# SSD, GLU and a top-1 mixture of experts on one core: the order of TensorE written out from GLU block 7 to the second expert's early rows

## Chip, cores and metric

The kernel runs on one core of a Trainium2 chip. The metric is the device time of one execution in microseconds; lower is better. Times come from the runs, durations and waits from one profiled execution.

## Reference

Three stages follow each other. A state-space layer (x, a, B, C in float32; 4 batches, 8 heads, 768 positions, head size 32, state size 16) gives 3072 tokens of 256 numbers. A gated layer follows, and then a mixture of eight experts in which each token goes to one expert:

```python
gate = 1.0 / (1.0 + np.exp(-(x @ w_gate)))
val = x @ w_val
x = (gate * val @ w_out).astype(np.float32)
...
expert_idx = np.argmax(logits, axis=1)
...
for e in range(E):
    mask = expert_idx == e
    h = np.maximum(x[mask] @ w1[e], 0.0)
    out[mask] = gate_w[mask, None] * (h @ w2[e])
```

w_gate and w_val are 256 x 1536, w_out is 1536 x 256, w1 is 256 x 1024 and w2 1024 x 256 for each expert. logits are cosine similarities of token and expert embedding over tau, gate_w is the softmax weight of the chosen expert.

## The kernel before

**Products.** Each float32 operand is split into a high and a low part (fp32r), and each product is three matmuls (high by high, high by low, low by high), so a contraction over 256 takes six.

**GLU steps.** The 3072 tokens are eight blocks (0 to 7) of 384. A block has twelve steps, one for each 128 columns of the hidden layer: step s is block s // 12, column tile s % 12. A step has a gate group (gate_step, six matmuls of 384 columns into bank 0, L583; ScalarE's tanh gives th, L587), a val group (val_step, six into bank 1, L597; VectorE gives pf, L601, ScalarE the high part of p, L604, VectorE its low part, L609) and an out group (out_step, nine of 264 columns into banks 2 to 4, L619), which uses the p of two steps earlier. In blocks 0 to 6 the state-space work of the next block stands among the steps.

**Routing.** After a block, route_a and route_b (VectorE, small instructions) find the expert of each token. route_rank counts with six tiny matmuls (L694, L695) how many earlier tokens go to the same expert, and needs ohb and car (L666, L671) from VectorE. route_c makes slot numbers from it (sli, L729), and GpSimd writes the block's rows, with the gate weight (row, L677), in three indirect DMAs into a table xs in DRAM (L735). For block 6 the rank is called in step 92 and the matmul of make_bump (L758) in step 94; for block 7 the rank is called in expert work, after up step 3 of the first segment.

**Expert work.** It has ten segments: segs[0] and segs[1] are the first 256 rows of experts 0 and 1 (the early rows, filled by blocks 0 to 6), segs[2] and segs[3] their next 192 rows, segs[4] to segs[9] the 448 rows of experts 2 to 7. seg_load brings the rows from xs on chip (xr, L832; it waits for the scatters) and copies gate weight and token number out of them on VectorE (gt, L839). seg_transpose turns them for one half k of the 256 columns (L855, bank 6 or 7), ScalarE and VectorE split the result (xt, L858 and L859). Eight up steps follow (L870: six matmuls into bank 0 or 1 in turn; ScalarE and VectorE give h, L874 and L875), and eight down steps (L884: six matmuls for segs[0] to segs[3], into banks 2 and 3 or 4 and 5). The results leave as yo (L919) with an indirect DMA. Weights of the experts come in 64 loads into three buffers stg (L798, SyncE's queue) and are split into we by ScalarE and VectorE (L806, L807); that runs from block 7 on.

**What sets the order.** Engines run their instructions in the order in which they stand. A list scheduler, with a timeline of its own, sets this order from the program, but within tc.manual_schedule the engines named keep the order of the code. Before, steps 28 to 83 (blocks 2, from its step 4, to 6) are such a region for TensorE (`"man": [[28, 84, ["PE"]]]` in the table of numbers); from step 84, block 7's first, the scheduler chooses. pend holds the up steps whose down step is still to come:

```python
for j, sg in enumerate(segs):
    ...
    for f in range(NFE):
        ...
        up_step(sg, f, hall[f] if last and f < NQ else None)
        ...
        pend.append((sg, f))
        while len(pend) > (kn("dlag", 2) if sg["ws"] != WS_A + WS_B else kn("dlag2", 1)):
            down_next()
        tf = kn("tfs", [2, 5, 5, 5, 5])[min(j, 4)]
        if f in (tf, tf + 1) and not last:
            seg_transpose(segs[j + 1], f - tf)
```

The table has "dlag": 1 and no "tfs", "dlag2", "m2" or "m2a", so the defaults in the code hold for these.

Of the kernel before, what the change touches and what calls it, by code (L numbers as in the profile page):

```python
# [3 lines left out]
def kn(n, d):  # L4
    return KN.get(n, d)
# [24 lines left out]
KD = DM // P  # L30
# [10 lines left out]
def kernel(  # L41
# [1102 lines left out]
    for s in range(S0, nstep + LAG2):  # L1144
        t, f = divmod(s, NF)
        if s == kn("trunc", 999):
            att_cm.__exit__(None, None, None)
            return
        if s == S0 + HOLD:
            hold.close()  # L1150
        for m in kn("man", []):
            if s == m[0]:
                region = tc.manual_schedule(engines={getattr(ET, e) for e in m[2]})
                region.__enter__()
            if s == m[1]:
                region.__exit__(None, None, None)
        if s == nstep - NF:
            close_att()
        if s > nstep - NF:
            with ExitStack() as es:  # L1160
                if kn("wl", 1) < 99:
                    for m in marks[min(s - kn("wl", 1), nstep - 1)]:
                        es.enter_context(tc.issue_after(m))
                weight_step()
        if s == nstep - 1:
            seg_load(segs[0])
            seg_load(segs[1])
        run(s, 0)
        drip()
        if s < nstep:  # L1170
            go(gate_step(t, f))
        run(s, 1)
        drip(2)
        gov = kn("gov", 999) <= s
        if s < nstep and not gov:
            go(val_step(t, f))
        run(s, 2)
        drip()
        while len(outs_done) <= s - (LAG if s < 26 else LAG2):
            out_step(*divmod(len(outs_done), NF))  # L1180
            outs_done.append(s)
        if s < nstep and gov:
            go(val_step(t, f))
        run(s, 3)
        drip(2)
# [21 lines left out]
                    seg_out(sg, i)  # L1207

    for j, sg in enumerate(segs):
        if j == kn("m2a", 0) and kn("m2", 0):  # L1210
            region = tc.manual_schedule(engines={ET.PE})
            region.__enter__()
        if j == kn("m2", 0) and j:
            region.__exit__(None, None, None)
        if j == 0:
            for k in range(KD):
                seg_transpose(sg, k)
            load_expert(2, main, slots[2])
        last = j == len(segs) - 1
        if last:  # L1220
# [1 line left out]
        for f in range(NFE):  # L1222
            if f == 0 and 2 <= j + 1 < len(segs):
                seg_load(segs[j + 1])
            up_step(sg, f, hall[f] if last and f < NQ else None)
            if j == 0:
                drip(10)
                if f == 3:
                    route_rank(NBLK - 1)
                if f == 4:  # L1230
                    route_c(NBLK - 1)
            pend.append((sg, f))
            while len(pend) > (kn("dlag", 2) if sg["ws"] != WS_A + WS_B else kn("dlag2", 1)):
                down_next()
            tf = kn("tfs", [2, 5, 5, 5, 5])[min(j, 4)]
            if f in (tf, tf + 1) and not last:
                seg_transpose(segs[j + 1], f - tf)
            weight_step()
        if last:
            while pend:  # L1240
                down_next()
            with tc.manual_schedule(engines={mybir.EngineType.PE}):
                for i in range(1, len(sg["ws"])):
                    for f in range(NFE):
                        down_tile(sg, f, i)
                    seg_out(sg, i)
# [52 lines left out]
```

## Time and profile before

| | |
|---|---|
| runs | 574.83, 579.59, 579.90 us (median 579.59) |
| profiled execution, its own time | 576.94 us |
| its span, first to last instruction | 575.2 us (1.7 us lie around it) |
| mean granted TensorE clock | 0.99 of 2.4 GHz |
| TensorE busy | 553.6 us |
| VectorE, ScalarE, GpSimd busy | 345.3, 282.4, 153.4 us |
| HBM traffic, mean | 130 GB/s |

All times in rows are microseconds from the first instruction. A matmul's duration is its passage through the array, in which several overlap: six gate matmuls of 0.34 us start within 1.05 us. So the time that a group takes is read from start to start. Busy counts these overlapping passages once.

### The profile page before, as it was taken

Reading aid. Unit: us, or ns where it says so; the run is one execution under the profiler, and the core shown is the slowest. Engines: PE = TensorE matmul, PEld = TensorE weight load, DVE = VectorE, ACT = ScalarE, POOL = GpSimd, SP = SyncE. Lnnn points to the kernel's source line nnn. Section 1 sums busy time; section 2 is a strip of 40 time slices with the busy share of each in tenths; the row PEclk is TensorE's granted clock in tenths of the full one; section 3 lists DMA queues with packets and bytes.
Section 4 is the critical chain, followed back from the end, with each engine's and each line's share of the span. In section 5 each row is a group of like instructions: output and inputs, shape, how many; then the busy total and the mean of one; then the engine's idle time right before and its main releaser. Section 6 shows DMA issues by size and latency. Waiting matters only on the chain. (4 is left out here: it accounts for less than half of the span.)

```text
span 575.2 us, 11363 instructions
## 1 busy us (share of the span) xinstructions
PE 553.6 (96%) x4160; PEld 521.1 (91%) x4160; DVE 345.3 (60%) x984; ACT 282.4 (49%) x712; POOL 153.4 (27%) x176
## 2 busy tenths in 40 slices
PE   9799999999999999999999999999999999999993
PEld 6689889999899999999999999999899889999993
DVE  4799966546747447547446447787376556543241
ACT  7566656355446446446445335673365444523220
POOL 3587843122432032231231020202221021121122
PEclk9799999999999999999999999999999999999998
DMA  8689799481561481471360131671365254200000
GB/s 282 172 291 268 213 238 288 144 186 52 175 175 37 120 199 41 135 175 38 92 147 3 33 106 37 204 225 59 120 189 179 74 172 149 87 29 10 18 26 30
DMA packets 74947, 75.02 MB, mean 130 GB/s; under 512 B 4971, under 2 KB 68659, under 8 KB 74888
## 3 DMA queue, kind: packets, MB, share of 16 engines
q1 hardware_dynamic: 72120, 67.91, 41.7%
q0 software_dynamic: 2688, 6.32, 3.3%
q8 instruction: 33, 0.54, 0.4%
q14 instruction: 26, 0.21, 0.1%
q10 hardware_dynamic: 80, 0.03, 0.0%
HBM read 58.53 MB, written 16.24 MB: 130 GB/s over the span
## 5 line engine op out<-in xcount | busy, mean ns | idle before, releaser
L619 PE MATMUL bk<-w,p 128*128 128x264 f32 x864 | 121.4, 285 | 0.0
L597 PE MATMUL bk<-xt,w 128*128 128x384 f32 x576 | 119.6, 343 | 1.0 <-DVE pf L601 1.0
L583 PE MATMUL bk<-xt,w 128*128 128x384 f32 x576 | 119.9, 343 | 0.0
L619 PEld LDWEIGHTS bk<-w,p 128*128 128x128 f32 x864 | 116.0, 188 | 0.4 <-issue 0.2
L597 PEld LDWEIGHTS bk<-xt,w 128*128 128x128 f32 x576 | 99.1, 189 | 3.1 <-DVE pf L601 1.2
L583 PEld LDWEIGHTS bk<-xt,w 128*128 128x128 f32 x576 | 98.6, 190 | 0.4
L604 ACT ACTIVATE p<-pf 128x384 fp32r<-128x384 f32 x96 | 50.0, 521 | 88.8 <-DVE pf L601 88.8
L870 PE MATMUL bk<-xt,we 128*128 128x448 f32 (+2 forms) x480 | 92.3, 330 | 0.0
L601 DVE SCALAR_TENSOR_TENSOR pf<-th,bk 128x384 f32<-128x384 f32 x96 | 53.0, 552 | 51.0 <-PE bk L597 44.9
L870 PEld LDWEIGHTS bk<-xt,we 128*128 128x128 f32 x480 | 78.0, 188 | 4.3
L587 ACT ACTIVATE th<-bk 128x384 f32<-128x384 f32 x96 | 46.7, 487 | 51.3 <-PE bk L583 51.2
L609 DVE TENSOR_TENSOR p<-pf,p 128x384 fp32r<-128x384 f32 x87 | 51.4, 590 | 32.6 <-ACT p L604 32.0
L874 ACT ACTIVATE h<-bk 128x448 fp32r<-128x448 f32 (+2 forms) x74 | 34.4, 464 | 71.9 <-PE bk L870 69.1
L920 POOL DMA_INDIRECT out_dram<-yo,gt x32 | 32.1, 1003 | 133.6 <-DVE yo L919 127.2
L875 DVE SCALAR_TENSOR_TENSOR h<-bk,h 128x448 fp32r<-128x448 f32 (+2 forms) x74 | 38.5, 521 | 38.3 <-ACT h L874 36.7
L312 POOL TENSOR_SCALAR_AFFINE_SELECT l<-l 128x512 f32<-128x512 f32 x42 | 27.4, 655 | 126.0 <-ACT l L308 108.2
L896 PE MATMUL bk<-h,we 128*128 128x448 f32 x240 | 58.0, 372 | 0.9 <-DVE h L875 0.9
L308 ACT ACTIVATE l<-cb,ncol 128x128 f32<-128x128 f32 x168 | 53.4, 390 | 9.6 <-DVE m L327 9.5
L735 POOL DMA_INDIRECT xs<-row,sli x24 | 25.4, 1057 | 89.5 <-DVE sli L729 29.5
L807 DVE TENSOR_TENSOR we<-stg,we 128x512 fp32r<-128x512 f32 x64 | 43.0, 685 | 9.2 <-ACT we L806 9.2
L896 PEld LDWEIGHTS bk<-h,we 128*128 128x128 f32 x240 | 43.6, 188 | 4.8 <-DVE h L875 1.6
L806 ACT ACTIVATE we<-stg 128x512 fp32r<-128x512 f32 x64 | 39.3, 627 | 16.8 <-PE bk L896 12.0
(171 smaller groups left out, 598.3 us busy)
## 6 DMA issues: line engine op xcount, KB each, us to landing
stg<-in_w_dram SPq DMA_DIRECT2D x64, 256.0 KB, 3.2
cb<-cum_d SPq DMA_DIRECT2D x21, 512.0 KB, 5.7
hl_d<-hl SPq DMA_DIRECT2D x7, 768.0 KB, 4.2
bts<-hl_d SPq DMA_DIRECT2D x21, 192.0 KB, 5.4
cts<-hl_d SPq DMA_DIRECT2D x42, 96.0 KB, 6.5
xs<-z SPq DMA_DIRECT2D x4, 903.0 KB, 8.7
raw<-in_w_val_dram SPq DMA_DIRECT2D x6, 512.0 KB, 5.6
xn<-in_x_dram SPq DMA_DIRECT2D x8, 384.0 KB, 5.3
```

Source lines behind the costliest of these rows:

```text
L308: A.activation(out=l[:, k, :], in_=cb[h], func=AF.Exp, bias=ncol[:, b, h, c:c + 1], scale=1.0)
L583: gi = T.matmul(gp, lhsT=wt["g", f // 2][:, wq, k, (f % 2) * P:(f % 2 + 1) * P], rhs=xts[t][:, xq, k, 0:TB], start=(i == 0), stop=(i == 3 ...
L587: A.activation(out=th, in_=gp, func=AF.Tanh, scale=0.5)
L597: T.matmul(vp, lhsT=wt["v", f // 2][:, wq, k, (f % 2) * P:(f % 2 + 1) * P], rhs=xts[t][:, xq, k, 0:TB], start=(i == 0), stop=(i == 3 * KD ...
L601: vi = V.scalar_tensor_tensor(out=pf, in0=ths.pop((t, f)), scalar=1.0, in1=vp, op0=ALU.add, op1=ALU.mult)
L604: ai = A.activation(out=p[:, 0, 0:TB], in_=pf, func=AF.Copy)
L609: pi = V.tensor_tensor(out=p[:, 1, 0:TB], in0=pf, in1=p[:, 0, 0:TB].bitcast(F32), op=ALU.subtract)
L619: T.matmul(oacc[t, i], lhsT=p[:, pq, i * P:(i + 1) * P], rhs=wt["o", f // 2][:, wq, f % 2, :], start=(f == 0 and j == 0), stop=(f == NF - ...
L806: A.activation(out=w[:, 0], in_=st[j][:, i], func=AF.Copy)
L807: V.tensor_tensor(out=w[:, 1], in0=st[j][:, i], in1=w[:, 0].bitcast(F32), op=ALU.subtract)
L870: T.matmul(hp[:, 0:W], lhsT=we[sg["e"], 0, f // 2][:, wq, k, (f % 2) * P:(f % 2 + 1) * P], rhs=sg["xt"][:, xq, k, 0:W], start=(i == 0), st ...
L896: T.matmul(sg["o", k][:, 0:W], lhsT=we[sg["e"], 1, f // 2][:, wq, f % 2, k * P:(k + 1) * P], rhs=sg["h", f][:, pq, 0:W], start=(f == 0 and ...
```

## The change

The region in which TensorE keeps the order of the code no longer ends at step 84; it begins at step 28 (S0) as before and ends ahead of segs[2], so it takes in block 7 and segs[0] and segs[1]. In that stretch code order now counts, and some of it is written in another way: the transposes of segs[0] stand in the loop of steps, behind the val group of the last step and ahead of the last two out groups; those of the next segment stand ahead of the down step in place of behind it; segs[2] is transposed at up steps 6 and 7 of segs[1] in place of 5 and 6; in segs[1] the down steps are two up steps behind in place of one, and one is caught up at its end. The other numbers were the defaults or the table's, and stay.


```diff
--- before.py
+++ after.py
@@ -1148,12 +1148,9 @@
             return
         if s == S0 + HOLD:
             hold.close()
-        for m in kn("man", []):
-            if s == m[0]:
-                region = tc.manual_schedule(engines={getattr(ET, e) for e in m[2]})
-                region.__enter__()
-            if s == m[1]:
-                region.__exit__(None, None, None)
+        if s == S0:
+            region = tc.manual_schedule(engines={ET.PE})
+            region.__enter__()
         if s == nstep - NF:
             close_att()
         if s > nstep - NF:
@@ -1176,6 +1173,9 @@
             go(val_step(t, f))
         run(s, 2)
         drip()
+        if s == nstep:
+            for k in range(KD):
+                seg_transpose(segs[0], k)
         while len(outs_done) <= s - (LAG if s < 26 else LAG2):
             out_step(*divmod(len(outs_done), NF))
             outs_done.append(s)
@@ -1207,14 +1207,9 @@
                     seg_out(sg, i)
 
     for j, sg in enumerate(segs):
-        if j == kn("m2a", 0) and kn("m2", 0):
-            region = tc.manual_schedule(engines={ET.PE})
-            region.__enter__()
-        if j == kn("m2", 0) and j:
+        if j == 2:
             region.__exit__(None, None, None)
         if j == 0:
-            for k in range(KD):
-                seg_transpose(sg, k)
             load_expert(2, main, slots[2])
         last = j == len(segs) - 1
         if last:
@@ -1230,12 +1225,14 @@
                 if f == 4:
                     route_c(NBLK - 1)
             pend.append((sg, f))
-            while len(pend) > (kn("dlag", 2) if sg["ws"] != WS_A + WS_B else kn("dlag2", 1)):
-                down_next()
-            tf = kn("tfs", [2, 5, 5, 5, 5])[min(j, 4)]
+            tf = (2, 6, 5, 5, 5)[min(j, 4)]
             if f in (tf, tf + 1) and not last:
                 seg_transpose(segs[j + 1], f - tf)
+            while len(pend) > (2 if j == 1 else 1):
+                down_next()
             weight_step()
+        if j == 1:
+            down_next()
         if last:
             while pend:
                 down_next()
```

TensorE at block 6's rank (L694, L695; six matmuls into bank 7). Rows begin with the val group of a step: bk1_5030 is step 86's before, bk1_5240 step 91's now. Before:

```order
L597 MATMUL bk1_5030<-xt_4441,w_479 128x384 x6
L619 MATMUL bk2_5043<-w_457,p_4977 128x264 x2
L619 MATMUL bk3_5047<-w_457,p_4977 128x264 x2
L619 MATMUL bk4_5051<-w_457,p_4977 128x264 x2
L619 MATMUL bk2_5043<-w_457,p_4977 128x264
L619 MATMUL bk3_5047<-w_457,p_4977 128x264
L619 MATMUL bk4_5051<-w_457,p_4977 128x264
L694 LDWEIGHTS tri_115
L694 MATMUL bk7_5269<-ohb_5009,tri_115 128x8
L695 LDWEIGHTS oneb_82
L695 MATMUL bk7_5269<-car_5010,oneb_82 128x8
L694 LDWEIGHTS tri_115
```

Now:

```order
L597 MATMUL bk1_5240<-xt_4441,w_711 128x384 x6
L619 MATMUL bk2_5042<-w_599,p_5170 128x264 x3
L619 MATMUL bk3_5046<-w_599,p_5170 128x264 x3
L619 MATMUL bk4_5050<-w_599,p_5170 128x264 x3
L694 LDWEIGHTS tri_115
L694 MATMUL bk7_5268<-ohb_5008,tri_115 128x8
L695 LDWEIGHTS oneb_82
L695 MATMUL bk7_5268<-car_5009,oneb_82 128x8
L694 LDWEIGHTS tri_115
L694 MATMUL bk7_5268<-ohb_5008,tri_115 128x8
L695 LDWEIGHTS oneb_82
L695 MATMUL bk7_5268<-car_5009,oneb_82 128x8
```

The rank matmuls stand five steps later, and all six together: before, gate group 87 (bk0_5065) stood behind the first three of the six.

TensorE at the transposes of segs[0] (bk6_5490 before, bk6_5445 now). bk0_5276 and bk1_5285 are gate and val group of step 92, bk0_5323 and bk1_5334 of step 93, bk1_5423 is val group 95, the last. Before:

```order
L583 MATMUL bk0_5276<-xt_4441,w_771 128x384 x6
L855 MATMUL bk6_5490<-ident_84,xr_5407 128x128 x2
L597 MATMUL bk1_5285<-xt_4441,w_825 128x384 x6
L619 MATMUL bk2_5043<-w_748,p_5250 128x264 x2
L619 MATMUL bk3_5047<-w_748,p_5250 128x264 x2
L619 MATMUL bk4_5051<-w_748,p_5250 128x264 x2
L619 MATMUL bk2_5043<-w_748,p_5250 128x264
L619 MATMUL bk3_5047<-w_748,p_5250 128x264
L619 MATMUL bk4_5051<-w_748,p_5250 128x264
L583 MATMUL bk0_5323<-xt_4441,w_771 128x384 x6
L597 MATMUL bk1_5334<-xt_4441,w_825 128x384 x6
L855 MATMUL bk6_5490<-ident_84,xr_5407 128x128 x2
```

Now:

```order
L583 MATMUL bk0_5414<-xt_4441,w_972 128x384 x6
L597 MATMUL bk1_5423<-xt_4441,w_916 128x384 x6
L619 MATMUL bk2_5042<-w_890,p_5342 128x264 x3
L619 MATMUL bk3_5046<-w_890,p_5342 128x264 x3
L619 MATMUL bk4_5050<-w_890,p_5342 128x264 x3
L855 MATMUL bk6_5445<-ident_84,xr_5406 128x128 x4
L619 MATMUL bk2_5042<-w_1117,p_5394 128x264 x3
L619 MATMUL bk3_5046<-w_1117,p_5394 128x264 x3
L619 MATMUL bk4_5050<-w_1117,p_5394 128x264 x3
L619 MATMUL bk2_5042<-w_1117,p_5432 128x264 x3
L619 MATMUL bk3_5046<-w_1117,p_5432 128x264 x3
L619 MATMUL bk4_5050<-w_1117,p_5432 128x264 x3
```

The two halves stood behind gate group 92 and val group 93; they now stand together behind out group 93, which follows val group 95.

TensorE in segs[1]: bk0 and bk1 with 128x256 (L870) are its up steps, bk4 and bk5 its down steps. bk6_5843 and bk6_5846 are the transposes of segs[2], bk7_6212 and bk7_6206 those of one half of segs[4]. Before, from up step 4 on:

```order
L870 MATMUL bk0_5810<-xt_5583,we1_4920 128x256 x6
L855 MATMUL bk6_5843<-ident_84,xr_5730 128x96 x2
L884 MATMUL bk4_5770<-we2_4923,h_5801 128x256 x2
L884 MATMUL bk5_5774<-we2_4923,h_5801 128x256 x2
L884 MATMUL bk4_5770<-we2_4923,h_5801 128x256
L884 MATMUL bk5_5774<-we2_4923,h_5801 128x256
L870 MATMUL bk1_5826<-xt_5583,we1_4920 128x256 x6
L855 MATMUL bk7_6212<-ident_84,xr_6046 128x128 x2
L884 MATMUL bk4_5770<-we2_4924,h_5817 128x256 x2
```

Now, from down step 1 on (bk0_5803 is up step 4):

```order
L884 MATMUL bk4_5779<-we2_4921,h_5750 128x256 x3
L884 MATMUL bk5_5783<-we2_4921,h_5750 128x256 x3
L870 MATMUL bk0_5803<-xt_5576,we1_4919 128x256 x6
L884 MATMUL bk4_5779<-we2_4922,h_5776 128x256 x3
L884 MATMUL bk5_5783<-we2_4922,h_5776 128x256 x3
L855 MATMUL bk7_6206<-ident_84,xr_6046 128x128 x2
L855 MATMUL bk7_6206<-ident_84,xr_6046 128x96 x2
L870 MATMUL bk1_5819<-xt_5576,we1_4919 128x256 x6
L884 MATMUL bk4_5779<-we2_4922,h_5794 128x256 x3
L884 MATMUL bk5_5783<-we2_4922,h_5794 128x256 x3
L870 MATMUL bk0_5835<-xt_5576,we1_4920 128x256 x6
L855 MATMUL bk6_5846<-ident_84,xr_5729 128x96 x2
```

The transposes of segs[4] stood behind up step 5 and those of segs[2] ahead of them, behind up step 4; now segs[4]'s stand ahead, behind the down step that follows up step 4, and segs[2]'s behind up step 6.

VectorE in the same place. h<-bk_5734, 5760, 5778, 5794, 5810 are up steps 0 to 4 of segs[1] before; 5733, 5743, 5769, 5787, 5803 are the same now. The first gt copy belongs to segs[2], the second to segs[3]. Before:

```order
L875 SCALAR_TENSOR_TENSOR h<-bk_5734,h 128x256
L919 TENSOR_SCALAR yo<-bk_5550,gt 128x256
L919 TENSOR_SCALAR yo<-bk_5554,gt 128x256
L875 SCALAR_TENSOR_TENSOR h<-bk_5760,h 128x256
L875 SCALAR_TENSOR_TENSOR h<-bk_5778,h 128x256
L839 COPY gt<-xr 96x4
L875 SCALAR_TENSOR_TENSOR h<-bk_5794,h 128x256
L839 COPY gt<-xr 96x4
L875 SCALAR_TENSOR_TENSOR h<-bk_5810,h 128x256
```

Now:

```order
L875 SCALAR_TENSOR_TENSOR h<-bk_5733,h 128x256
L919 TENSOR_SCALAR yo<-bk_5549,gt 128x256
L875 SCALAR_TENSOR_TENSOR h<-bk_5743,h 128x256
L919 TENSOR_SCALAR yo<-bk_5553,gt 128x256
L839 COPY gt<-xr 96x4
L875 SCALAR_TENSOR_TENSOR h<-bk_5769,h 128x256
L875 SCALAR_TENSOR_TENSOR h<-bk_5787,h 128x256
L839 COPY gt<-xr 96x4
L875 SCALAR_TENSOR_TENSOR h<-bk_5803,h 128x256
```

The gt copy of segs[2] stood behind the h of up step 2 and now stands ahead of it.

## Rows read from the trace of the kernel before

**Rows 1.** The page's part 1: busy time, share of the span, instructions.

```profile
PE 553.6 (96%) x4160; PEld 521.1 (91%) x4160; DVE 345.3 (60%) x984; ACT 282.4 (49%) x712; POOL 153.4 (27%) x176
```

**Rows 2.** Busy time by stretch: PE, PEld, DVE, ACT, POOL; granted clock, DMA share, GB/s.

```profile
350.00:370.00 20.00, 20.00 (x137) 19.74 (x136) 17.41 (x69) 12.80 (x30) 2.93 (x3) 1.00 0.41 126
370.00:390.00 20.00, 19.30 (x132) 18.75 (x131) 15.92 (x32) 14.75 (x31) 0.49 (x1) 1.00 0.76 235
390.00:410.00 20.00, 18.73 (x162) 18.31 (x161) 11.96 (x65) 6.58 (x20) 4.89 (x5) 1.00 0.25 80
```

**Rows 3.** Waits of TensorE: who for whom, us in total, times, longest.

```profile
PE bk L855 <- DMA xr<-xs: 2.0, 3, 0.7
```

**Rows 4.** Timeline of TensorE: start, us, instructions merged, idle before and its releaser.

```profile
327.94 1.23 PE L583 MATMUL bk<-xt,w 128*128 128x384 f32 x6
...
331.15 0.18 PE L694 MATMUL bk<-ohb,tri 128*128 128x8 bf16 x1
...
331.32 1.31 PE L583 MATMUL bk<-xt,w 128*128 128x384 f32 x6
...
344.77 2.23 PE L619 MATMUL bk<-w,p 128*128 128x264 f32 x17
...
369.92 1.21 PE L583 MATMUL bk<-xt,w 128*128 128x384 f32 x6
370.96 1.20 PE L597 MATMUL bk<-xt,w 128*128 128x384 f32 x6
...
373.09 1.23 PE L583 MATMUL bk<-xt,w 128*128 128x384 f32 x6
375.02 0.44 PE L855 MATMUL bk<-ident,xr 128*128 128x128 f32 x2 [0.70 <-DMA xr<-xs]
...
390.39 1.58 PE L870 MATMUL bk<-xt,we 128*128 128x256 f32 x12
...
396.03 0.18 PE L694 MATMUL bk<-ohb,tri 128*128 128x8 bf16 x1
...
396.98 0.88 PE L870 MATMUL bk<-xt,we 128*128 128x256 f32 x6
...
405.45 0.87 PE L870 MATMUL bk<-xt,we 128*128 128x256 f32 x6
406.89 0.38 PE L855 MATMUL bk<-ident,xr 96*128 96x96 f32 x2 [0.57 <-DMA xr<-xs]
...
407.84 0.87 PE L870 MATMUL bk<-xt,we 128*128 128x256 f32 x6
409.41 0.41 PE L855 MATMUL bk<-ident,xr 128*128 128x128 f32 x2 [0.69 <-DMA xr<-xs]
```

**Rows 5.** Timeline of VectorE, same columns.

```profile
372.27 0.55 DVE L601 SCALAR_TENSOR_TENSOR pf<-th,bk 128x384 f32<-128x384 f32 x1 [0.22 <-PE bk L597]
375.00 0.17 DVE L839 COPY gt<-xr 128x4 f32<-128x4 f32 x1 [2.17 <-DMA xr<-xs]
...
394.37 0.15 DVE L671 TENSOR_TENSOR car<-car,ohb 128x8 bf16<-128x8 bf16 x1
...
398.05 0.16 DVE L729 TENSOR_TENSOR sli<-sl,df 128x3 int32<-128x3 f32 x1
...
406.87 0.17 DVE L839 COPY gt<-xr 96x4 f32<-96x4 f32 x1 [2.49 <-DMA xr<-xs]
406.94 0.41 DVE L875 SCALAR_TENSOR_TENSOR h<-bk,h 128x256 fp32r<-128x256 f32 x1
```

**Rows 6.** Timeline of GpSimd: the scatters of block 6 and block 7.

```profile
364.28 0.97 POOL L735 DMA_INDIRECT xs<-row,sli  x1 [26.41 <-DVE row L677]
...
366.85 0.98 POOL L735 DMA_INDIRECT xs<-row,sli  x1 [0.31 <-issue]
...
398.97 1.00 POOL L735 DMA_INDIRECT xs<-row,sli  x1 [27.48 <-DVE h L875]
```

**Rows 7.** Timeline of SyncE's DMA queue: loads of segs[0] and segs[1].

```profile
370.98 0.88 SPq L832 DMA_DIRECT2D xr<-xs  x2
```

## Prediction

> **What bounds the kernel now.** I read the page first: TensorE is busy for 553.6 us, 96% of the span [rows 1], so time can only be won where TensorE stands still. The table of busy time by stretch then says how much that is where the order changes: nothing from 350 to 370, 0.70 us from 370 to 390 and 1.27 us from 390 to 410 [rows 2]. The list of waits names the cause: the transposes of expert rows (L855) wait three times for the loads of these rows, 2.0 us in all [rows 3]. The timeline of TensorE shows the places, and what each really costs from start to start. The gate group of step 92 begins at 373.09 and such a group takes 1.04 (the step before: 369.92 to 370.96), yet the transpose behind it begins at 375.02: 0.89 us lost. From 396.98 to 405.45 lie twelve groups of an expert without a stop, 0.706 each, so 405.45 to 406.89 loses 0.73, and 407.84 to 409.41 loses 0.86 [rows 4]. Sum: 2.48 us, 0.4% of the run. Everything else that TensorE does here is a fixed amount of matmuls, and the change keeps them all.
>
> The sum below is made against the profiled execution, 576.94 us. The median of the three runs is 579.59, their lowest 574.83. The middle between profiled execution and median, 578.3, is what I compare with at the end.
>
> **What goes.** All three waits, 2.48 us, if nothing takes their place. Also some changes between kinds of matmul: the gate group right behind the rank matmuls lasts 1.31 (331.32) where 1.23 is usual (373.09), so a break costs about 0.08 [rows 4]. The new order has four breaks fewer (the transposes of segs[0] in one piece and not two, those of each half of segs[4] likewise, block 6's rank matmuls no longer split by a gate group): 0.32 us. That out groups are issued x3 and no longer x2 and x1 gains nothing: a step of the scheduler's order takes 3.17 us (369.92 to 373.09), a written-out step of block 6 3.21 (327.94 to 331.15) [rows 4]. In all 2.80 us can go.
>
> **What comes: segs[0]'s transposes.** They now stand behind the out group of step 93. When does TensorE get there? Out group 81 ends after 9 of the 17 matmuls from 344.77, which take 2.07, so at 345.87. Eight steps of 3.21 lead to block 6's rank matmuls at 371.55; these cost 0.25 (331.15 to 331.32, and a break), four more steps 12.84, and the one matmul of the bump 0.1: 384.74 [rows 4]. When are the rows there? The rank now decides late. VectorE has the slot numbers (sli) behind the val group of step 92, which starts at 372.84; its pf follows 1.31 later (370.96 to 372.27 [rows 4, 5]) and lasts 0.55, so sli begins at 374.7. GpSimd starts the scatter 0.92 later (398.05 to 398.97): 375.6 [rows 5, 6]. From the first scatter to the rows on chip took 10.72 us for block 6 (364.28 to 375.00) and 7.90 for block 7 (398.97 to 406.87) [rows 5, 6]. So the rows come at 383.5 or 386.3, and TensorE waits for 0 or 1.6 us. I take 0.3, near the quick case: the slow one had its load among fourteen weight loads (DMA share 0.76 from 370 to 390 [rows 2]), while now 25 of the 30 stand ahead of it and are done.
>
> The Trainium skill (DMA: Bandwidth & Descriptors, section "Anatomy of one DMA") gives a DMA issued by GpSimd 2.0 us plus its bytes over 436 GB/s. The scatter writes 132 KB, so an estimate by that page is 2.3 us from issue to completion, and with it the load would go out in time, this wait be 0 and the net 0.3 lower. The trace does not agree: block 6's third scatter begins at 366.85 and the load that waits for it at 370.98, 4.1 us [rows 6, 7]. The measured times decide, and the term stays at 0.3.
>
> A second cost hangs on it. VectorE copies gate weights and indices (gt) out of these rows in its own order, and stands still until they arrive (2.17 us at 375.00 [rows 5]). Behind this copy now stands pf of step 95, which the last out group needs by way of three instructions of about 0.5 each; TensorE has 1.5 us of transposes and out group 94 ahead of it. Bounds 0 to 0.7, taken 0.3.
>
> **What comes: block 7's rank and segs[2], segs[4].** The rank matmuls move from behind up step 5 to behind up step 3 of segs[0]. In the old order TensorE came to its stop (405.45 and a group, 406.15) 10.1 us after the rank (396.03) [rows 4]. In the new one I count from the rank on: the rank 0.25, two transposes 0.24 (406.89 to 407.84 less a group), then sixteen groups to up step 4 of segs[1] at 0.706 each (above), 11.8 us. That helps by 1.7. But three things move against it. First, the scatter also needs the gate weight (row, L677), and this now stands behind the h of up step 4, two groups after the rank: 1.9 to the end of that group, about 1.0 until ScalarE and VectorE have made its h, 0.5 for five short instructions and 0.9 to GpSimd's start put the scatter at rank + 4.3, in place of 2.94 (396.03 to 398.97 [rows 4, 6]). Second, the gt copy of segs[2] stands one h earlier: before h of up step 2 of segs[1] and no longer before that of step 3. Up step 4 writes the bank that this h reads. The rows come at 4.3 + 7.9, copy and h take 0.6 more (406.87 to 406.94 + 0.41 [rows 5], and the way to TensorE): up step 4 can start at rank + 12.8, TensorE is there at 11.8. Bounds 0 (scatter at 2.94) and 3.8 (scatter at 4.3 and block 6's 10.72); taken 1.0. Third, the first transposes of segs[4] stand two groups behind that, ahead of segs[2]'s own, and their load comes last: 10.44 after the scatter (398.97 to 409.41 [rows 4, 6]), so at rank + 14.7, and the second half of the load, which comes still later, is wanted at once. TensorE is there at 12.8 and two groups, 14.2: 0.5 and a little, taken 0.8, bounds 0.2 and 1.4.
>
> That rank itself waits for VectorE's car is not to be feared: in the old order car was done 4.1 us after the last out group (390.39 to 394.37 + 0.15 [rows 4, 5]), and six groups and two transposes, 4.5 us, now lie between. At the seam to segs[2], where the scheduler mixes its first up steps into the end of the region, the first down group stands right behind its up step: 0.15, bounds 0 and 0.5.
>
> **The sum.** Comes: 0.3 + 0.3 + 1.0 + 0.8 + 0.15 = 2.55, with ends at 0.2 and 8.0. Goes: 2.80. Net -0.2, between -2.6 and +5.2. Against the profiled execution 576.7, against the median 579.4, against their middle 578.1.
>
> **The rivals.**
> *The waits go and nothing follows them.* If both scatters land as quickly as block 7's and the gate weight is no later than now, only 0.2 is left of what comes: net -2.6, 575.7. For it: scatter and load take 7.9 us in one of two cases. Against: block 6's rank now comes eight steps into block 7, with four steps left to the transposes.
> *The copy of segs[2] holds up VectorE.* If block 7's scatter and load take what block 6's took, 10.72, up step 4 of segs[1] waits 3.8 and the net is 0.3 + 0.3 + 3.8 + 0.8 + 0.15 - 2.80 = +2.6, 580.9: slower. It decides from 8.5 us of scatter and load on: 4.3 + 8.5 + 0.6 - 11.8 is the 1.6 us of the two waits that it replaces. Against: by then few weight loads are left (share 0.25 from 390 to 410 [rows 2]).
> *The runs that last longer do so here.* Two of the three runs took 579.59 and 579.9, the third 574.83. If the excess of the two lies in these same waits and the new order covers it, every run takes what the third took, less most of the 2.48 us: 572.8, faster by more than 1%. Nothing in the one profile shows it.
>
> **How the numbers follow.** The forecast, a net between -1.5 and +1.2, has 0.53; the first rival 0.25, the second 0.16, the third 0.06. A measurement of this kernel can tell about 1% (5.8 us) from no change. Forecast and first two rivals stay within that, but for an end of the second; the runs' own spread of 5 us takes a little more on either side: faster 0.08, no change 0.88, slower 0.04. The range for 8 in 10 goes from a bit under the lowest run to the slower rival: 574.0 to 581.0.
>
> **What would show it.** Right: the three transpose waits gone from the places of [rows 4]; L855 waiting at most once for about 0.3 behind step 95's val; in segs[1] a gap of about 1 us ahead of up step 4, with VectorE idle on gt, and another ahead of segs[4]'s transposes; steps of block 7 at 3.21. Wrong: no gap in segs[1] (the scatter is not later than I say), a gap of over 2 us there, or a wait of the rank on car. The forecast falls if stops move into block 7's steps themselves, where I expect none.

## The result: 0.95% slower, and the profile after

The changed kernel takes 582.34 us (median of 8 runs, 580.04 to 583.72) where the one before takes 576.55 beside it (8 runs, 574.83 to 579.9): a ratio of 1.0095, 95% interval 1.0073 to 1.0118. The forecast was 578.1, its range ended at 581.0.

| | before | after |
|---|---|---|
| profiled execution, us | 576.94 | 583.02 |
| its span | 575.2 | 581.3 |
| start of the val group of step 83 | 343.73 | 344.00 |
| from there to the end of the span | 231.47 | 237.30 |
| mean granted clock of TensorE | 0.990 | 0.981 |

Up to step 83 almost nothing moved (0.27 us); the rest of the loss, 5.83 us, lies behind it. TensorE's timeline, same columns as [rows 4], shows where:

```profile
383.78 1.27 PE L619 MATMUL bk<-w,p 128*128 128x264 f32 x9
388.19 0.51 PE L855 MATMUL bk<-ident,xr 128*128 128x128 f32 x2 [3.13 <-DMA xr<-xs]
389.63 0.69 PE L855 MATMUL bk<-ident,xr 128*128 128x128 f32 x2 [0.93 <-DVE xt L859]
389.97 4.31 PE L619 MATMUL bk<-w,p 128*128 128x264 f32 x18
394.08 2.12 PE L870 MATMUL bk<-xt,we 128*128 128x256 f32 x12
396.03 1.12 PE L884 MATMUL bk<-we,h 128*128 128x256 f32 x6
396.99 0.87 PE L870 MATMUL bk<-xt,we 128*128 128x256 f32 x6
...
406.10 1.58 PE L870 MATMUL bk<-xt,we 128*128 128x256 f32 x12
...
410.36 0.86 PE L884 MATMUL bk<-we,h 128*128 128x256 f32 x6
411.94 0.98 PE L870 MATMUL bk<-xt,we 128*128 128x256 f32 x6 [0.72 <-DVE h L875]
412.75 0.87 PE L884 MATMUL bk<-we,h 128*128 128x256 f32 x6
413.58 0.41 PE L855 MATMUL bk<-ident,xr 128*128 128x128 f32 x2
414.17 0.38 PE L855 MATMUL bk<-ident,xr 96*128 96x96 f32 x2 [0.18 <-DMA xr<-xs]
```

The out group of step 93 begins at 383.78, and such a group takes 1.09 from start to start, so TensorE is ready for segs[0]'s transposes at 384.87. They start at 388.19. Their second half starts not 0.14 later but at 389.63, with VectorE named as the one waited for, and out group 94 at 389.97. In e10b (below), where neither rows nor VectorE are waited for, all four transposes take 0.36 to the next group; here they take 1.78, so 1.42 is lost. Then 18 matmuls take 4.11 us, where two out groups take 2.18, the up steps 1.95 where the same twelve matmuls take 1.42 at 406.10, and the down step 0.96 for 0.71. From 396.99 on the pace is the old one. The list of TensorE's waits [rows 3] has become:

```profile
PE bk L855 <- DMA xr<-xs: 3.3, 2, 3.1
...
PE bk L855 <- DVE xt L859: 0.9, 1, 0.9
...
PE bk L870 <- DVE h L875: 0.7, 1, 0.7
```

and the table of busy time by stretch [rows 2] tells why whole groups became slow:

```profile
386.00:388.00 2.00, 0.00 (x0) 0.00 (x0) 0.00 (x0) 0.00 (x0) 0.00 (x0) 1.00 0.77 222
388.00:390.00 2.00, 0.88 (x5) 0.57 (x5) 1.65 (x5) 0.80 (x2) 0.00 (x0) 0.61 1.00 315
390.00:394.00 4.00, 4.00 (x20) 4.00 (x19) 1.38 (x6) 0.90 (x3) 0.00 (x0) 0.50 0.58 195
394.00:396.00 2.00, 2.00 (x14) 2.00 (x13) 1.08 (x7) 1.00 (x4) 0.00 (x0) 0.69 0.00 0
```

TensorE does nothing from 386 to 388, still at a granted clock (the last column but two) of 1.00. Right behind the stop the clock falls from the 2.4 to the 1.2 GHz level: the mean of 0.61 from 388 to 390 puts the fall at about 388.4, and from 390 to 394 it is 0.50. The mean of 0.69 from 394 to 396 puts the way back to 1.00 at about 395.2. In segs[1], the up step behind the down step of 410.36 is due at 411.06 and starts at 411.94 (0.88 late); the first transposes of segs[4] lose about 0.6.

So the loss adds up from rows: 3.32 (standing for rows) + 1.42 (between the halves) + 2.7 (half clock: 1.93 + 0.53 + 0.25) + 0.88 + 0.6 = 8.9, less the 2.80 that was to go: 6.1, where 5.83 was measured.

Why were the rows late? These are the rows of GpSimd, VectorE and SyncE's queue on that chain, which answer to [rows 5 to 7]:

```profile
375.93 2.97 POOL L735 DMA_INDIRECT xs<-row,sli  x1 [37.80 <-DVE we L807]
...
380.53 1.15 POOL L735 DMA_INDIRECT xs<-row,sli  x1 [0.30 <-issue]
...
403.61 0.99 POOL L735 DMA_INDIRECT xs<-row,sli  x1 [17.90 <-DVE row L677]
```

```profile
375.01 0.16 DVE L729 TENSOR_TENSOR sli<-sl,df 128x3 int32<-128x3 f32 x1
375.08 1.29 DVE L807 TENSOR_TENSOR we<-stg,we 128x512 fp32r<-128x512 f32 x2
376.29 0.56 DVE L609 TENSOR_TENSOR p<-pf,p 128x384 fp32r<-128x384 f32 x1
376.76 1.29 DVE L807 TENSOR_TENSOR we<-stg,we 128x512 fp32r<-128x512 f32 x2
377.96 0.55 DVE L601 SCALAR_TENSOR_TENSOR pf<-th,bk 128x384 f32<-128x384 f32 x1
...
388.16 0.17 DVE L839 COPY gt<-xr 128x4 f32<-128x4 f32 x1 [2.50 <-DMA xr<-xs]
```

```profile
374.66 5.71 SPq L798 DMA_DIRECT2D stg<-in_w_dram  x7
385.39 0.88 SPq L832 DMA_DIRECT2D xr<-xs  x2
```

VectorE's sli comes at 375.01 and the first scatter starts at 375.93, 0.3 later than predicted. But it lasts 2.97 where every scatter of [rows 6] lasts 0.97 to 1.00, so the third starts at 380.53. The load goes out 4.86 behind that (4.13 in [rows 6, 7]) and its rows are there at 388.16: 12.23 us from first scatter to rows, more than either case of before (7.90 and 10.72). Against the quick case of before, 7.90, that is 4.33 more, in two parts of like size: from the first scatter to the third 4.60 in place of 2.59, and from the third to the issue of the load 4.86 in place of 2.55 (401.56 to 404.11 in before, block 7). From that issue to the rows it is 2.77, as there (2.76). Seven weight loads went out from 374.66 on, beside the scatters; the DMA share is 0.62 from 380.53 to 385.39, where it was 0.29 from 401.56 to 404.11. Block 7's scatter starts 4.28 behind the rank (399.33 to 403.61), as predicted (4.3).

### The profile page after: what moved, and what is told of

It reads as the page before. It is cut to its first block, busy times and chain, and to the rows that moved or that the text cites. A ratio compares the mean times of both kernels' runs of the same rounds, so it can differ in the third digit from the quotient of the medians.

```text
span 581.3 us, 11363 instructions
## 1 busy us (share of the span) xinstructions
PE 557.2 (96%) x4160; PEld 525.1 (90%) x4160; DVE 347.6 (60%) x984; ACT 281.6 (48%) x712; POOL 155.4 (27%) x176
## 5 line engine op out<-in xcount | busy, mean ns | idle before, releaser
L619 PE MATMUL bk<-w,p 128*128 128x264 f32 x864 | 123.7, 289 | 0.0
L619 PEld LDWEIGHTS bk<-w,p 128*128 128x128 f32 x864 | 118.7, 193 | 0.2 <-issue 0.2
L870 PE MATMUL bk<-xt,we 128*128 128x448 f32 (+2 forms) x480 | 93.1, 331 | 0.7 <-DVE h L875 0.7
L870 PEld LDWEIGHTS bk<-xt,we 128*128 128x128 f32 x480 | 78.6, 190 | 5.3 <-DVE h L875 0.9
L735 POOL DMA_INDIRECT xs<-row,sli x24 | 27.5, 1147 | 91.4 <-DVE we L807 37.8
```

The lines of the kernel that those rows point to most:

```text
L619: T.matmul(oacc[t, i], lhsT=p[:, pq, i * P:(i + 1) * P], rhs=wt["o", f // 2][:, wq, f % 2, :], start=(f == 0 and j == 0), stop=(f == NF - ...
L870: T.matmul(hp[:, 0:W], lhsT=we[sg["e"], 0, f // 2][:, wq, k, (f % 2) * P:(f % 2 + 1) * P], rhs=sg["xt"][:, xq, k, 0:W], start=(i == 0), st ...
```

## The experiments

All times are medians; a ratio is against the kernel before on the same chip. The last column is the profiled execution from the start of step 83's val group to the end of the span; it is one execution of each kernel, and leaves out the early part of the kernel: that varied by 4.5 us between profiles though no edit touches it (342.91 to 347.42).

| kernel | us | ratio, 95% interval | step 83 to end |
|---|---|---|---|
| before | 576.55 to 578.96 | | 231.47 |
| after | 582.34 | 1.0095 [1.0073, 1.0118] | 237.30 |
| e1_rank4 | 582.95 | 1.0063 [1.0035, 1.0091] | 234.39 |
| e2_fill | 585.70 | 1.0102 [1.0041, 1.0163] | 239.02 |
| e3_banks | 582.83 | 1.0089 [1.0064, 1.0114] | 237.24 |
| e4_both | 580.40 | 1.0031 [1.0006, 1.0056] | 234.34 |
| e5_gates | 580.48 | 1.0031 [0.9998, 1.0064] | 232.24 |
| e6_region | 578.95 | 1.0012 [0.9988, 1.0036] | 234.48 |
| e10_gates0 | 578.80 | 0.9999 [0.9977, 1.0022] | 231.29 |
| e10b | 576.79 | 0.9970 [0.9944, 0.9997] | 231.38 |
| e13_before_gates | 577.72 | 0.9993 [0.9973, 1.0012] | 231.69 |
| e8_tlate | 587.27 | 1.0141 [1.0082, 1.0200] | 240.28 |
| e11_tlate_gates | 583.35 | 1.0078 [1.0048, 1.0108] | 234.85 |
| e7_quiet | 586.38 | 1.0121 [1.0064, 1.0178] | 239.62 |

(e9_junk and e12_noload stand here for one row of the profile each; each has a single run, 586.38 and 586.65.)

### What the stop ahead of segs[0] consists of: e1, e3, e4, e2

**e1_rank4**: block 6's rank and slots three steps earlier.

```diff
-            at(e0 + 7, 0, route_rank, t)
-            at(e0 + 7, 3, route_c, t)
+            r0 = e0 + (4 if t == NBLK - 2 else 7)
+            at(r0, 0, route_rank, t)
+            at(r0, 3, route_c, t)
```

> The changed kernel with block 6's rank and slot numbers called three steps earlier (step 89 in place of 92), all else the same. Theory A (late rows): the scatter starts about 9.6 us earlier, the rows of segs[0] are there when TensorE comes to its transposes, so the wait of 3.1 us, and the half clock behind it, go: 583.0 less 3.3 less 2.7, about 577, with a granted clock of 0.99 and L855 waiting for xr by less than 0.7 us in all. Theory B (the loss comes from writing the order out, wherever the rank stands): within 1 us of the changed kernel, 582.

**e3_banks**: segs[0]'s two halves in banks 6 and 7, like the longer segments. **e4_both**: both edits.

```diff
-        if W > 2 * P:
+        if W > 2 * P or sg is segs[0]:
             tp = bank(6 + k, (P, CAP))
```

> The changed kernel with the two halves of segs[0]'s transposes in banks 6 and 7 in place of one bank. Theory: the second half waited 0.93 us for VectorE to read the first half out of the same bank, since both now stand together; with two banks this wait goes, and the time falls by about 1 us to 581.3; the wait for the rows and the half clock stay. Rival (the second half waits for the rows as well, not for the bank): no change, 582.3.

> Both: block 6's rank in step 89 and two banks for segs[0]'s transposes. If the late rows with their half clock (6.0 us) and the shared bank (1.3 us) are what the change lost, about 575.5 to 576, no slower than the kernel before; if part of the loss lies elsewhere, 577 or more.

Measured, TensorE's timeline of e1_rank4:

```profile
386.77 1.27 PE L619 MATMUL bk<-w,p 128*128 128x264 f32 x9
387.88 0.38 PE L855 MATMUL bk<-ident,xr 128*128 128x128 f32 x2
391.61 0.44 PE L855 MATMUL bk<-ident,xr 128*128 128x128 f32 x2 [3.35 <-DVE xt L859]
391.81 2.43 PE L619 MATMUL bk<-w,p 128*128 128x264 f32 x18
```

of e3_banks:

```profile
390.42 1.11 PE L855 MATMUL bk<-ident,xr 128*128 128x128 f32 x4 [3.90 <-DMA xr<-xs]
391.18 4.31 PE L619 MATMUL bk<-w,p 128*128 128x264 f32 x18
```

and of e4_both:

```profile
386.58 0.60 PE L855 MATMUL bk<-ident,xr 128*128 128x128 f32 x4
387.29 0.51 PE L619 MATMUL bk<-w,p 128*128 128x264 f32 x2
388.07 2.74 PE L619 MATMUL bk<-w,p 128*128 128x264 f32 x16 [0.27 <-DVE p L609]
...
408.69 0.97 PE L870 MATMUL bk<-xt,we 128*128 128x256 f32 x6 [1.21 <-DVE h L875]
...
410.87 0.41 PE L855 MATMUL bk<-ident,xr 128*128 128x128 f32 x2 [0.51 <-DMA xr<-xs]
```

In e1_rank4 the rows are there and the first half starts without a wait, 1.11 behind its out group (386.77). But the second half stands 3.35 us for VectorE's copy of the first, because both lie in one bank: that copy stands behind splits of weights that are still on their way. In e3_banks the gap between the halves is gone, the wait for rows (3.90) and the half clock (4.31 for 18 matmuls) stay, and almost nothing is won: 237.24. Part of that is a longer landing: from block 6's third scatter to the issue of the load it took 5.55 us there (4.86 in after), so the rows came later. The place itself, from the start of out group 93 to the first up step, tells the shares: 10.30 us in after (383.78 to 394.08), 10.04 in e3_banks, 7.30 in e1_rank4, 5.19 in e4_both. Only both edits take the stop away; by the ratios e4_both is 0.6% shorter than after, with intervals that do not overlap. Rank and bank are two separate causes: with one of them mended the other still makes TensorE stand. The times that the theories gave, 577 (e1), 581.3 (e3) and 575.5 to 576 (e4), were all missed; e4_both came out where its expectation has part of the loss elsewhere.

In the last column e1_rank4 and e4_both are alike (234.39 and 234.34), for what e4_both gains here it loses again behind it. It loses 0.5 where out group 94 waits for p of step 94 (5.19 is still 1.3 more than the 3.86 of e10b, below), 1.2 ahead of up step 4 of segs[1] and 0.7 ahead of segs[4]'s transposes, the second and third of which are terms of the prediction.

**e2_fill**: nine bfloat16 matmuls without use (128x512, into a free bank) ahead of segs[0]'s transposes.

> The changed kernel with nine matmuls of ones (128 x 512, bf16, into the free bank 7) ahead of the transposes of segs[0], in the time that TensorE waits for the rows; they add work and compute nothing that is used. The rows come as late as in the changed kernel. Theory A1 (the clock falls because TensorE stood still for 3 us): it now stands still for about 1.2 us, the 18 matmuls of the last two out groups take 2.2 us and not 4.1, granted clock 0.99, time 2.7 us below the changed kernel, about 580. Rival A2 (the low clock comes from something else): time as the changed kernel, 582 to 583, 4.1 us for those 18 matmuls.

Measured: the nine fill 386.27 to 389.95, just the wait (the rows are there at 389.92), at a granted clock of 1.00. The second half then stands 1.71 us for VectorE, and after this stop the clock is at 0.50 from 392 to 394 all the same; out groups 94 and 95 take 3.61 (392.43 to 396.04). A bridge of matmuls does not pay here: it moved the fall of the clock to the next stop. From out group 93 to the third up step it is 13.27 us (385.16 to 398.43), in after 13.21 (383.78 to 396.99), and the ratio is that of after; what the last column has more, 1.72, lies behind that place.

### The stops in segs[1]: e5, e6, e10, e13

**e5_gates** (on e4_both): gt copies of segs[2] and later are issued behind the h of their segment's last up step. **e6_region**: besides, TensorE's written order goes on to the end of segs[3].

```diff
+            if f == NFE - 1 and j > 1:
+                with tc.issue_after(sg["hv"]):
+                    seg_gates(sg)
...
-        if j == 2:
+        if j == 4:
             region.__exit__(None, None, None)
```

> Block 6's rank three steps earlier and segs[0]'s transposes in two banks, as in e4_both; besides, VectorE's gt copies of segs[2] and all later segments stand at the end of their segment, behind the h of its last up step. Theory (the copy holds up the h that up step 4 of segs[1] waits for): the 1.21 us ahead of that up step goes to 0.3 or less. But TensorE then comes about 1.0 us earlier to the first transposes of segs[4], whose rows come no sooner, so their waits grow from 0.7 to about 1.7: the time is that of e4_both within 0.5 us (580.0 to 580.5). Rival (the h waits for something else): the gap ahead of up step 4 stays at about 1.2.

> As e5_gates, and TensorE's written order goes on to the end of segs[3], so that the transposes of segs[4] stand behind up steps 5 and 6 of segs[3] and not in segs[1]. Theory (rows that come late are the whole rest of the loss): neither up step 4 nor a transpose in segs[1] waits over 0.3 us, and the time falls by 1.2 + 0.7 from that of e4_both, to about 578.5; against before that is a ratio of 0.998 to 1.002. Rival (the wait moves on to segs[2]'s own transposes, or to the seam at the end of segs[3]): 580 or more, with a stop of 1 us or more at one of these places.

Measured: in e5_gates the gap ahead of up step 4 is gone, and the waits of segs[4]'s transposes grow from 0.7 to 1.1 (0.81 + 0.29), with one more of 1.03 at 433.14; the median is that of e4_both, as expected, though the one profiled execution is 2.1 shorter in the last column. So it was the copy, and the next late thing stood right behind it. In e6_region no instruction of TensorE in segs[1] waits; a new stop of 2.7 us stands in segs[4]:

```profile
438.79 0.47 PE L890 MATMUL bk<-we,h 128*96 128x256 f32 x2 [2.74 <-ACT h L879]
```

ScalarE's h for it begins at 438.42, behind a weight split that waited 4.03 us for its load. My reading: the late copies held the row buffers, of which there are three, so the next row load stood in SyncE's queue until 428.70 and eight weight loads behind it. The next kernel tries that.

**e10_gates0**: as e6_region, with the copies behind the h of the segment's first up step (`f == 0`). **e10b**: segs[0]'s and segs[1]'s copies moved likewise. **e13_before_gates**: the kernel before with all copies so, and nothing else.

> As e6_region, but the gt copies of segs[2] and later stand behind the h of their segment's first up step and not of its last: in e6_region they held the row buffers so long that the next row load, and behind it the weight loads, came late, and TensorE stood 2.7 us at the start of segs[4]. Theory: that stop goes, no new one comes, and the time is 576.5 to 578.0, a ratio to before of 0.996 to 1.000. Rival (the weights come late because of the written order itself): the stop stays over 1.5 us and the time at 579.

> As e10_gates0, and the gt copies of segs[0] and segs[1] moved behind the h of their first up step as well, so that pf and p of step 95 no longer stand behind them. Theory: out group 94 is no longer broken after two matmuls (0.5 us in e4_both), so 0.3 to 0.6 less than e10_gates0: 576.0 to 577.7. Rival (p comes late for another reason, the weight splits ahead of it): same as e10_gates0 within 0.2.

> Before, with the gt copies of all segments behind the h of their first up step, as in e10b; nothing else. If these copies alone bring what e10b brings, this is as fast as e10b, about 576.8 where before has 579.0 (ratio 0.995 to 0.999). If e10b needs the written order as well, this is as before within 0.3% (578 to 580): in before the three waits of 2.48 us are for rows and not for a copy.

Measured: in e10_gates0 1.14 is left of that stop (one execution of each: the slowest run of e6_region, the fastest of e10_gates0). That speaks for the copies as part of its cause and not all of it, but does not show it. The kernel is where before is. e10b is the only version that is shorter than before, 0.3% with an interval that ends just under 1, so by little if at all beyond the noise; it still stands 1.27 at that place. Its timeline at the place where after stood still:

```profile
383.60 1.27 PE L619 MATMUL bk<-w,p 128*128 128x264 f32 x9
384.71 0.60 PE L858 MATMUL bk<-ident,xr 128*128 128x128 f32 x4
385.07 2.56 PE L619 MATMUL bk<-w,p 128*128 128x264 f32 x18
387.46 1.58 PE L873 MATMUL bk<-xt,we 128*128 128x256 f32 x12
```

The transposes start 1.11 behind their out group, and the two out groups and two up steps run in a piece: what the change meant to do, with the rank three steps earlier, two banks, later copies and a longer written order. The later copies alone (e13_before_gates) change nothing that can be measured (0.9973 to 1.0012). That interval overlaps with the one of e10b (0.9944 to 0.9997), so whether e10b's 0.3% is there at all, and whether it needs the written order, is not shown.

### The clock: e8, e11

**e8_tlate**: after, with segs[0]'s transposes behind the out group of step 95. **e11_tlate_gates**: besides, all gt copies behind the h of their segment's first up step.

```diff
-        if s == nstep:
-            for k in range(KD):
-                seg_transpose(segs[0], k)
...
             outs_done.append(s)
+        if s == nstep + 1:
+            for k in range(KD):
+                seg_transpose(segs[0], k)
```

> After, with segs[0]'s transposes behind the out group of step 95 and no longer ahead of that of step 94. Nothing changes when the rows come. Theory (standing still for 3 us is what let the clock fall): the wait shrinks by the two out groups, 2.2 us, to about 1.1; the granted clock stays at 1.00; behind the transposes the first up step waits about 1.3 for the second half's xt: 582.3 - 2.2 + 1.3 - 2.7 = 578.7. Rival (the clock falls for another reason, such as the loads that run there): 0.50 for some 6 us all the same, and 581 or more.

> As e8_tlate (segs[0]'s transposes behind the out group of step 95; rank at its place in after), and all gt copies behind the h of their segment's first up step. In e8_tlate VectorE stood on the gt copy and out group 95 waited 2.81 us for it. Theory: now both out groups run at once, TensorE comes to the transposes about 1.1 us before the rows and stands again about 0.9 and 1.3 us for the halves' copies; the granted clock stays 1.00, and the time is 578 to 580. Rival (the clock falls with these shorter stops too): 0.50 for some microseconds and 581 or more.

Measured: e8_tlate is the slowest of all, and its expectation missed a queue. VectorE stands on the gt copy until the rows are there, and p of step 95 behind it, so the last out group waits for the same rows:

```profile
391.67 2.50 PE L619 MATMUL bk<-w,p 128*128 128x264 f32 x9 [2.81 <-ACT p L604]
```

The clock falls there as well (0.50 from 392 to 398). In e11_tlate_gates, where VectorE is free, both out groups run while the rows travel; its named stops there are 0.28, 0.93 and 0.22, and the granted clock stays at 1.00:

```profile
388.00:390.00 2.00, 1.91 (x15) 1.58 (x13) 0.96 (x3) 0.52 (x1) 0.00 (x0) 1.00 0.77 225
390.00:392.00 2.00, 1.07 (x9) 0.70 (x8) 1.59 (x9) 1.80 (x7) 0.00 (x0) 1.00 0.95 289
```

Against after this is 2.45 us shorter from step 83 on (234.85), though its transposes in segs[1] wait 1.71; its median did not come down (583.35, expected 578 to 580), so that the clock's share of the time rests on the rows of after alone.

### The scatter that takes three times as long: e7, e9, e12

**e7_quiet**: no weight steps at 90, 91 and 92. **e9_junk**: five VectorE operations on a scratch tile behind the gate weight of block 7. **e12_noload**: expert 1's weights are not loaded, its splits read expert 0's last ones again (so its rows come out with other weights), and four splits are held back until right behind block 6's sli.

> After, but without the weight steps at 90, 91 and 92: what they would load (8 of the 30 loads) goes out behind the load of segs[0]'s rows, so that block 6's scatter has few loads beside it. Theory (the loads beside it made the scatter slow): the first scatter takes about 1.0 us and not 2.97, from scatter to rows 8 to 9 us and not 12.2, the wait ahead of segs[0]'s transposes is under 0.7 and the granted clock stays at 1.00 there; weights come up to 12 us later, so other waits may arise in the expert steps, and the total says little (579 to 586). Rival (late rows come of the scatter itself or its place): 2.97 and about 12 stay.

> After, with five VectorE operations on a scratch tile (128x704, both operands and result on chip, about 0.9 us each) behind the gate weight of block 7, where few loads run. They are of the kind of L807, which runs while block 6's first scatter lasts 2.97 us. Theory V (a scatter that begins while VectorE is in such an operation stands until it can get in between): at least one of block 7's three scatters, one that begins inside a scratch operation, lasts 1.2 us or more and the lengthening is what was left of that operation. Theory L (loads beside it lengthen a scatter): all three last 0.97 to 1.02 as in after. The total rises by 1 to 3 us and tells nothing.

> After, without the loads of expert 1's weights (their place is taken by a second use of expert 0's last ones, so expert 1's rows come out with other weights), so that few loads run beside block 6's scatter; and four of VectorE's weight operations (L807 in after) are held until right behind sli, so that VectorE has two-operand work without a gap when that scatter begins, as in after. Theory V (the scatter stands behind VectorE's two-operand operations): the first scatter lasts 1.5 to 3.0 us although nothing is loaded beside it. Theory L (loads lengthen it): it lasts 0.97 to 1.02. The total tells nothing.

Measured: e7_quiet has a first scatter of 0.97 and a wait for rows of 1.30; from scatter to rows it is still 10.40 us (377.53 to 387.93), since the landing takes 4.91, and the second half then stands 3.58 for VectorE. So a scatter of the usual length would not have been enough. But the run moved VectorE's splits together with the loads, so it does not tell the two apart. In e9_junk the three scatters happened to begin within 0.1 us of an operation's end or beside another kind, and took 0.97 to 0.99: it tells nothing. e12_noload does tell. GpSimd, VectorE, and the stretch in question:

```profile
378.05 3.57 POOL L741 DMA_INDIRECT xs<-row,sli  x1 [40.34 <-DVE sli L688]
```

```profile
377.21 2.49 DVE L816 TENSOR_TENSOR we<-stg,we 128x512 fp32r<-128x512 f32 x4
379.62 0.55 DVE L609 TENSOR_TENSOR p<-pf,p 128x384 fp32r<-128x384 f32 x1
380.09 0.68 DVE L816 TENSOR_TENSOR we<-stg,we 128x512 fp32r<-128x512 f32 x1
380.69 0.55 DVE L601 SCALAR_TENSOR_TENSOR pf<-th,bk 128x384 f32<-128x384 f32 x1
```

```profile
380.00:381.00 1.00, 0.88 (x5) 0.54 (x4) 1.00 (x3) 0.03 (x1) 1.00 (x1) 1.00 0.00 0
```

From 380 to 381 no byte moves (DMA share 0.00), and the scatter that began at 378.05 goes on until 381.62 (3.57 us, beyond the 1.5 to 3.0 expected). VectorE has operations with two operands on chip back to back from 377.21 until pf at 380.69, which reads one operand from a bank. The last of them ends at 380.77, the scatter 0.85 later. The same sum holds in after: the last split ahead of pf ends at 378.05, the scatter at 378.90. In e2_fill, e3_banks, e8_tlate and e11_tlate_gates, with the same order on VectorE, the first scatter took 2.96 each time, though the early part's shifts put the loads elsewhere (DMA share from 376 to 378: 0.36 in e3_banks, 0.85 in after). The kernel before had shown it on a small scale in its blocks 1 to 4, which [rows 6] leaves out: there the second scatter of each block lasts 1.27 to 1.30, and ends 0.85 after the operation that makes the low part of p, which has two operands on chip. In block 3:

```profile
247.15 1.27 POOL L735 DMA_INDIRECT xs<-row,sli  x1 [0.30 <-ACT p L604]
```

```profile
247.02 0.56 DVE L609 TENSOR_TENSOR p<-pf,p 128x384 fp32r<-128x384 f32 x1 [0.84 <-ACT p L604]
```

Of the 384 scatters of rows in the sixteen traces 102 last over 1.1 us, and every one of these ends 0.82 to 0.88 after the end of such an operation. So their length is set by VectorE, not by the loads. What the loads do lengthen is the landing, from the third scatter to the load's issue: 4.86 us in after and 3.54 to 6.00 for block 6 in every kernel that loads weights beside it, against 2.59 in e12_noload (383.20 to 385.79) and 2.52 to 2.91 for block 7.

The Trainium skill ("SBUF — State Buffer", section "Who interferes with whom") says that a VectorE instruction with two SBUF inputs contends with a GpSimd instruction that reads SBUF, and calls the ports that they share an exclusive lock. The trace agrees with the standing. How long a scatter stands when such operations follow one another is another matter: the first scatter of after and of e12_noload waited out a whole row of them, but the third of after (1.15 us, 380.53) and the first of e4_both (1.32 us) got in after one, with the next right behind it. Why there and not here stays open.

## Why the prediction was wrong

- *segs[0]'s transposes, taken 0.3, bounds 0 to 1.6.* This is the step that failed. TensorE's arrival was right (384.87 for 384.74) and so was sli (375.01 for 374.7). From scatter to rows I took the two cases of before as bounds, 7.90 and 10.72; it took 12.23, and the wait was 3.32. Two things made it so. The change put the first scatter into a row of VectorE operations with two operands on chip, and it lasted 2.97. The two cases of before could not show this: block 7's first scatter had no such operation at its start, block 6's began 0.09 before the end of one (364.28, the operation ends at 364.37) and was not held up by the two splits behind it, and both lasted about 1 us. And the reason for leaning to the quick case failed: 25 of the 30 weight loads stood ahead, but seven of them went out beside the scatters, and the landing took 4.86 where the quick case had 2.55.
- *What hangs on that wait* was priced for pf alone; two more things were put at nothing without a reason. The two halves of the transposes lie in one bank: I counted their standing together as a gain of breaks, where it cost 1.42 with VectorE late. And the clock: 2.7 us more than the matmuls' old pace. These 4.1 are the other half of the miss; neither shows where the rows come in time and two banks are used (e4_both).
- *pf of step 95 behind gt, taken 0.3.* Not to be seen in after, since the stop covers it; 2.81 in e8_tlate, where nothing covers it. It is the same late rows, seen from VectorE. The 0.5 in e4_both is another thing: there gt is copied by 378.92, and p of step 94 stands behind weight splits.
- *Up step 4 of segs[1] behind the copy of segs[2], taken 1.0:* 0.88, and e5_gates, built on e4_both, shows that it is the copy. *segs[4]'s transposes, taken 0.8:* 0.6. Scatter at rank + 4.28, predicted 4.3; scatter to rows 7.78, predicted 7.9. All of these terms hold.
- *What goes, 2.80:* the three waits are gone from their places and the steps of block 7 do run at 3.20 without a stop; the sum above closes with it to 0.3.
- *The sides.* The slower rival put the place of the loss into segs[1] and its price at +2.6; it came at segs[0], at +5.8. The chance of 0.04 for slower than 1% was far too small for a kernel with a wait whose length hangs on a chain of several engines and queues; the ratio itself, 1.0095, ends just within that 1%.

The prediction's estimate of 2.3 us for a scatter, from the figures of the Trainium skill ("DMA: Bandwidth & Descriptors", section "Anatomy of one DMA"), is far off beside weight loads (4.13 in before, 4.86 here) and near where there are few (2.59 in e12_noload, 2.55 behind block 7 in before).

## What to carry to other kernels

When an order is written out and a wait moved, price the chain that ends in it anew at its new place: who runs beside each link there, and not what the link took before. Beside each wait ask what hangs on it if it is longer than thought: a shared bank, another engine that waits for the same data in its own order (the gt copy), the clock. Give late data slack first (here, the rank three steps earlier and the gt copies behind the h of the first up step), then fix the order.

## What the hardware showed that was not expected

- A scatter from GpSimd that stands for VectorE operations with two operands on chip ends 0.82 to 0.88 us after the end of one (102 scatters): 1.27 to 1.30 us behind a single one, 2.97 and 3.57 behind a row, in place of 0.97. At which of several it gets in was not settled.
- From the third scatter to the load that waits for it: 3.54 to 6.00 us beside weight loads, 2.52 to 2.91 with few.
- TensorE's granted clock fell to 0.50 right behind a stop of 3.1 us (after), with about 2.7 us lost behind it, and in one of 3.9 (e3_banks), but also after 1.71 us in e2_fill, and not after 3.35 in e1_rank4, where it stayed at 1.00 (window 390 to 394). The length of one stop alone does not decide it; what does was not settled.
